# A norm step behind later PSUM copies, Q and K chunks in alternation, and a logit group three steps later, in a one-core transformer kernel

## The chip, the cores and the metric

The kernel runs on one core of one Trainium2 chip. The metric is device time in microseconds (us), lower is better. All times are medians of several executions.

The engines are called as the profile calls them. PE is TensorE (matrix products), DVE is VectorE (elementwise work, sums along a row), ACT is ScalarE (activation functions, here also the copies out of PSUM and most of the layer norm), POOL is GpSimd, and SP is SyncE, which issues DMAs. PSUM is the memory that TensorE writes to.

## The reference, cut to what matters

The input is 2048 tokens of width 1024 in bf16. Two layers, A and B, are applied twice with the same weights.

```python
x = A_x
for _ in range(2):                                    # written out in the original
    x = x + attention(layernorm(x), wqkv, wo)         # 32 heads of 32, window of 8 keys, dilation 2
    x = x + (relu(n @ W_gate) * (n @ W_up)) @ W_down  # n = layernorm(x), F = 3584
```

Attention looks only at the eight keys at distances 0, 2, ..., 14, so its logits are not a large matrix product. They are elementwise products of Q with eight shifted copies of K, summed over each head's 32 features.

## The kernel before

The kernel works on blocks of 512 tokens: four in each of two passes, numbered 0 to 7 in time. Every piece of work is an event with a nominal time. The events are sorted by it and emitted in that order, so that each engine is given its own instructions in this order. The nominal time is therefore a position in a queue, not a wait:

```python
for _, _, f in sorted((at, i, f) for i, (at, f) in enumerate(events)):
    f()
```

`tc.issue_after(ins)` puts an instruction behind `ins` in that order; TensorE's matmul groups are kept in sequence by it. One pool of six PSUM buffers, `acc`, serves the results of all projections.

The layer norm of most blocks runs on ScalarE in two events for each tile of 128 tokens. GpSimd computes a power between two of the ScalarE steps:

```python
def stats(t):
    ...
    nc.scalar.activation(xn, xt[:], ACT.Square, accum_out=sq)
    nc.scalar.activation(xn, xt[:], ACT.Identity, accum_out=sx)
    ...                                                              # three small ScalarE steps -> vpe
    nc.gpsimd.tensor_tensor(rstd, vpe, neg_half[:, 0:1], op=ALU.pow) # variance ** -0.5
    nc.scalar.activation(mr, sx, ACT.Copy, scale=-1.0 / D)
    nc.scalar.activation(nb, mr, ACT.Identity, scale=rstd)           # the bias step: needs GpSimd's result

def apply(t):
    nc.scalar.activation(hold["xn"][:, t, :], x_tiles[b * TPB + t][:], ACT.Identity,
                         scale=hold["st"][:, t, 4:5], bias=hold["st"][:, t, 6:7])
```

The Q and K projections run two Q chunks ahead of K. ScalarE copies each chunk out of PSUM. GpSimd copies the halo, the 14 last tokens of the block before:

```python
QK_ORDER = [("q", 0), ("q", 1)]
for c in range(2, KC):
    QK_ORDER += [("q", c), ("k", c - 2)]
QK_ORDER += [("k", KC - 2), ("k", KC - 1)]
...
    nc.scalar.copy(q[:], acc[:])                 # or k
    ...
    nc.gpsimd.tensor_copy(k[:, 0:HALO], khalo[n - 1][:, c, :])      # L362, blocks after the first
    nc.gpsimd.tensor_copy(khalo[n][:, c, :], k[:, BLK:BLK + HALO])  # L363
```

In block 0 VectorE multiplies each Q chunk with eight shifts of its K chunk (`prod`, L391), and TensorE sums each product over the heads with a selection matrix (the logit matmuls, `L<-prod,sel`). VectorE then computes the softmax, whose exponential (`d<-d`) is ScalarE's. In the later blocks VectorE also sums the eight products (`ac`, `t`, and at last `s`), and TensorE needs one group of eight logit matmuls (`L<-s,sel`). In block 1 that group and its softmax lie inside the gated unit of block 0:

```python
ev.append((t_gu0 + 48.1, red1))                  # the logit matmuls of block 1
ev.append((t_gu0 + 48.2, lambda: softmax(1)))
...
spread(pv_steps(1), at + 58.0, 5.5)              # value products of block 1, at = t_gu0
ev.append((at + 105.0, store_o(1)))              # to DRAM, and back transposed: oT
ev.append((at + 105.1, load_o(1)))
```

The gated unit takes 28 steps of a gate group and an up group, eight matmuls each. ScalarE applies ReLU to the gate (`r`, three buffers), and VectorE multiplies (`hT`). In the down projection four accumulators are filled for one half of the columns, VectorE adds them to the residual (`x<-dacc,x`), and the second half follows. With six `acc` buffers the third accumulator of the second half needs one that these additions free.

## Time and profile before

Three runs took 1642.17 to 1643.27 us, median 1643.09. The profiled execution spans 1640.5 us from its first instruction to its last.

The first part of the profile's page lists each engine's busy time, share of the span and number of instructions:

```profile
PE 1617.3 (99%) x7527; PEld 777.7 (47%) x7576; DVE 1061.3 (65%) x923; ACT 508.1 (31%) x1047; POOL 268.0 (16%) x220
```

TensorE is busy all the time that the profile can see. What is left to win are its holes. The table of waits names what TensorE waited for. Its columns are total microseconds, number of times, and the longest time:

```profile
PE tp L295 <- DVE xn_first L277: 9.1, 1, 9.1
PE L L118 <- DVE s L429: 1.9, 1, 1.9
PE L L118 <- DVE prod L391: 1.7, 2, 0.9
PE tp L295 <- ACT xn_first L292: 1.2, 2, 0.9
PE acc_v L118 <- ACT xnT_first L299: 1.1, 1, 1.1
PE acc_u L118 <- ACT r L550: 1.0, 1, 1.0
PE acc_u L118 <- DVE hT L551: 0.7, 1, 0.7
PE acc_g L118 <- ACT r L550: 0.2, 1, 0.2
```

The lines with `tp` and `acc_v` are the head of the kernel, before 15.3 us: the first norm and its transposes. The change doesn't touch them. The other five lines are six holes with 5.62 us in all:

| hole at (us) | size (us) | stage | waits for |
|---|---|---|---|
| 63.73, 69.54 | 0.85, 0.89 | end of block 0's Q/K stage | VectorE's products |
| 165.96 | 0.69 | gated unit of block 0 | a PSUM buffer that VectorE's hT frees |
| 171.55, 174.48 | 0.25, 1.04 | gated unit of block 0 | PSUM buffers that ScalarE's ReLU frees |
| 202.76 | 1.90 | gated unit of block 0 | the sum s for block 1's logit group |

Why is ScalarE late with a ReLU when it is busy for only 31% of the span? Its timeline shows it. The columns are start, duration, engine, line, operation and tile; the brackets hold the idle time before it and what ended that:

```profile
66.32 0.29 ACT L232 ACTIVATE st_a<-st_a 128x1 f32<-128x1 f32 x1 [1.64 <-POOL st_a L230]
66.52 0.57 ACT L358 CAST k<-acc_k 128x512 bf16<-128x512 f32 x1
...
75.67 1.04 ACT L446 ACTIVATE d<-d 128x1024 f32<-128x1024 f32 x1
...
158.40 0.60 ACT L550 ACTIVATE r<-acc_g 128x512 bf16<-128x512 f32 x1
166.17 0.29 ACT L232 ACTIVATE st_a<-st_a 128x1 f32<-128x1 f32 x1 [7.17 <-POOL st_a L230]
```

L232 is the bias step. It handles 128 numbers in 0.29 us, but at 166.17 it had held up ScalarE for 7.17 us and at 66.32 for 1.64 us, and ReLUs and copies stood behind it. The Trainium skill, "Perfetto Trace Analysis", section "Tensor Engine Instruction (MATMUL, LD_WEIGHTS)", says that ScalarE, VectorE and GpSimd take their instructions strictly in order. This trace agrees: nothing overtook the bias step in those 7.17 us. GpSimd's timeline of the same kernel says why its results were late:

```profile
63.69 2.60 POOL L230 TENSOR_TENSOR st_a<-st_a,neg_half 128x1 f32<-128x1 f32 x1
...
165.44 0.20 POOL L362 COPY k<-kh 128x14 bf16<-128x14 bf16 x1 [21.64 <-DVE ac L417]
165.59 0.55 POOL L230 TENSOR_TENSOR st_a<-st_a,neg_half 128x1 f32<-128x1 f32 x1
```

At 165.44 a halo copy had waited 21.64 us for VectorE, and the power (L230) stood behind it in GpSimd's queue. At 63.69 the power itself took 2.60 us instead of 0.55.

The last two excerpts of before are of VectorE and TensorE. The last product of block 0 starts at 67.17, after a wait for ScalarE's copy of K. The sum s ends at 202.71, and TensorE waited 1.90 us for it:

```profile
67.17 2.31 DVE L391 TENSOR_TENSOR prod<-q,k 128x4096 bf16<-128x4096 bf16 x1 [1.30 <-ACT k L358]
...
200.43 2.28 DVE L429 TENSOR_TENSOR s<-ac,t 128x2048 bf16<-128x2048 f32 x1
```

```profile
198.65 1.89 PE L118 MATMUL acc_u<-xnT_b,w_u 128*128 128x512 bf16 x8
200.47 0.40 PE L118 MATMUL L<-s,sel 128*32 128x512 bf16 x4
202.76 0.40 PE L118 MATMUL L<-s,sel 128*32 128x512 bf16 x4 [1.90 <-DVE s L429]
```

Groups of eight matmuls that run back to back start 1.727 us apart, yet one is drawn 1.89 us long. The same section of the Trainium skill says that the profiler estimates the end of a matmul.

### The profile page before, as it was taken

To read this page: it belongs to the slowest core of one execution; us is meant where nothing else is said; L and a number is where in the kernel's file an instruction comes from. 1 tells how busy PE (TensorE), PEld (TensorE's weight loads), DVE (VectorE), ACT (ScalarE), POOL (GpSimd) and SP (SyncE) were. 2 spreads that over 40 slices of the span, in tenths; PEclk is the share of its full clock that TensorE was granted. 3 is DMA by queue.
4 is the path that set the end of the run, shared out by engine and by line. 5 is a ranking of instruction groups with operands and counts; after the bars stand their busy time and mean duration, and the time that the engine had idled before them with its cause. 6 is when DMAs were issued, how large, how long until landed. Compare 5 with 4: busy or idle time off the path is not lost.

```text
span 1640.5 us, 18585 instructions
## 1 busy us (share of the span) xinstructions
PE 1617.3 (99%) x7527; PEld 777.7 (47%) x7576; DVE 1061.3 (65%) x923; ACT 508.1 (31%) x1047; POOL 268.0 (16%) x220
## 2 busy tenths in 40 slices
PE   7999999999999999999999999999999999999999
PEld 4554345444554445444454444544445444444444
DVE  3699998977298945949369492794928948211211
ACT  5833412424231512415134151340513411131110
POOL 1320205301052102101052010520105100000000
PEclk9999999999999999999999999999999999999999
DMA  8559566746657475774847748577485774755451
GB/s 291 98 152 252 164 180 205 192 146 180 205 177 210 134 199 167 202 200 154 228 153 192 174 154 231 176 183 205 150 225 167 200 213 154 206 154 180 154 164 67
DMA packets 371222, 296.81 MB, mean 181 GB/s; under 512 B 142400, under 2 KB 351296, under 8 KB 370240
## 3 DMA queue, kind: packets, MB, share of 16 engines
q1 hardware_dynamic: 370848, 295.10, 62.7%
q8 instruction: 59, 0.97, 0.3%
q10 hardware_dynamic: 288, 0.52, 0.1%
q14 instruction: 27, 0.22, 0.0%
HBM read 256.77 MB, written 21.00 MB: 169 GB/s over the span
## 4 chain that ended last, share of the span: by engine, by line
PE 93%; DVE 3%; ACT 2%; DMA 1%; issue 1%; POOL 0%; SPq 0%; DVEq 0%; ACTq 0%
PE dacc L118 23%; PE acc_g L118 22%; PE acc_u L118 22%; PE acc_wo L118 7%; PE acc_v L118 6%; PE acc_k L118 6%; PE acc_q L118 6%; DVE t L417 1%; DVE ac L429 1%; DMA x<-in_A_x_dram 1%; DMA v_d<-vT 1%; ACT xn_a L225 0%; ACT xn_a L226 0%; DVE prod L391 0%; PE L L118 0%
## 5 line engine op out<-in xcount | busy, mean ns | idle before, releaser
L118 PE MATMUL acc_u<-xnT_b,w_u 128*128 128x512 bf16 x1792 | 423.3, 379 | 1.7 <-ACT r L550 1.0
L118 PE MATMUL acc_g<-xnT_b,w_g 128*128 128x512 bf16 x1792 | 423.4, 379 | 0.2 <-ACT r L550 0.2
L118 PE MATMUL dacc<-w_d,hT 128*128 128x512 bf16 x1759 | 386.3, 379 | 1.7
L551 DVE TENSOR_TENSOR hT<-acc_u,r 128x512 bf16<-128x512 f32 x224 | 153.3, 687 | 307.4 <-PE acc_u L118 296.1
L550 ACT ACTIVATE r<-acc_g 128x512 bf16<-128x512 f32 x224 | 132.4, 594 | 695.4 <-PE acc_g L118 675.5
L118 PEld LDWEIGHTS <-w_u 128*128 128x128 bf16 x1792 | 175.3, 98 | 213.5 <-issue 2.3
L118 PEld LDWEIGHTS <-w_g 128*128 128x128 bf16 x1792 | 174.7, 98 | 213.0 <-issue 3.3
L118 PEld LDWEIGHTS <-hT 128*128 128x128 bf16 x1792 | 175.3, 98 | 211.4
L419 DVE TENSOR_TENSOR t<-q,k 128x2048 f32<-128x2048 bf16 x84 | 191.7, 2290 | 9.7 <-ACT k L358 7.0
L429 DVE TENSOR_TENSOR ac<-ac,t 128x2048 f32<-128x2048 f32 x84 | 191.7, 2283 | 0.5
L363 POOL COPY kh<-k 128x14 bf16<-128x14 bf16 x64 | 83.8, 1315 | 439.4 <-ACT k L358 439.4
L578 DVE TENSOR_TENSOR x<-dacc,x 128x512 bf16<-128x512 f32 x64 | 42.5, 687 | 164.7 <-PE dacc L118 164.7
L481 DVE TENSOR_TENSOR pv<-a,vhm 128x4096 bf16<-128x4096 bf16 x64 | 145.2, 2282 | 0.0
L230 POOL TENSOR_TENSOR st_b<-st_b,neg_half 128x1 f32<-128x1 f32 x29 | 62.8, 2169 | 319.7 <-ACT st_b L229 319.7
L118 PE MATMUL acc_wo<-w_o,oT 128*128 128x512 bf16 x496 | 111.0, 379 | 0.8
L230 POOL TENSOR_TENSOR st_a<-st_a,neg_half 128x1 f32<-128x1 f32 x32 | 45.9, 1434 | 334.0 <-ACT st_a L229 331.6
L362 POOL COPY k<-kh 128x14 bf16<-128x14 bf16 x48 | 70.2, 1463 | 65.4 <-DVE t L419 43.8
L118 PEld LDWEIGHTS <-oT 128*128 128x128 bf16 x512 | 50.0, 98 | 60.4
L482 DVE TENSOR_TENSOR pv<-pv 128x2048 bf16<-128x2048 bf16 x64 | 77.5, 1215 | 0.2
L319 ACT CAST vT<-acc_v 128x512 bf16<-128x512 f32 x64 | 37.5, 586 | 73.9 <-PE acc_v L118 73.9
L225 ACT ACTIVATE xn_b<-x 128x1024 bf16<-128x1024 bf16 x29 | 30.3, 1045 | 93.1 <-DVE x L526 93.1
L354 ACT CAST q<-acc_q 128x512 bf16<-128x512 f32 x64 | 37.5, 585 | 69.3 <-PE acc_q L118 69.3
(125 smaller groups left out, 1207.5 us busy)
## 6 DMA issues: line engine op xcount, KB each, us to landing
w_g<-in_B_W_gate_dram SPq DMA_DIRECT2D x56, 1024.0 KB, 7.0
w_u<-in_B_W_up_dram SPq DMA_DIRECT2D x56, 1024.0 KB, 5.4
w_d<-in_B_W_down_dram SPq DMA_DIRECT2D x48, 1024.0 KB, 5.8
w_o<-in_A_wo_dram SPq DMA_DIRECT2D x16, 1024.0 KB, 7.3
vhm<-v_d SPq DMA_DIRECT2D x32, 284.0 KB, 6.8
v_d<-vT SPq DMA_DIRECT2D x8, 1024.0 KB, 10.3
oT<-o_d SPq DMA_DIRECT2D x32, 256.0 KB, 4.3
w_d<-in_B_W_down_dram SPq DMA_DIRECT2D x16, 512.0 KB, 3.9
```

The costliest lines, as they stand in the source:

```text
L118: tail_pe[0] = nc.tensor.matmul(*args, **kwargs).ins
L230: nc.gpsimd.tensor_tensor(rstd, vpe, neg_half[:, 0:1], op=ALU.pow)
L319: nc.scalar.copy(st["vT"][:, c, :], acc[:])
L362: nc.gpsimd.tensor_copy(k[:, 0:HALO], khalo[n - 1][:, c, :])
L363: nc.gpsimd.tensor_copy(khalo[n][:, c, :], k[:, BLK:BLK + HALO])
L419: nc.vector.tensor_tensor(t[:], i0, i1, op=ALU.mult)
L429: nc.vector.tensor_tensor(o, ac[:], t[:], op=ALU.add)
L481: nc.vector.tensor_tensor(tt[:], a_bc, v_sh, op=ALU.mult)
L482: nc.vector.tensor_tensor(tt[:, 0:4], tt[:, 0:4], tt[:, 4:8], op=ALU.add)
L550: nc.scalar.activation(r[:], acc[:], ACT.Relu)
L551: nc.vector.tensor_tensor(hold["hT"][:, j, :], accs["u"][:], r[:], op=ALU.mult)
L578: nc.vector.tensor_tensor(xs, ac[t], xs, op=ALU.add)
```

## The change

The change has three parts, called A, B and C below. No work goes or comes.

- **A, the norm.** The bias step leaves `stats` and goes next to `apply`. Both are placed behind the latest ScalarE copy out of PSUM or ReLU, and at later times. A wait for GpSimd should then hold up fewer copies.
- **B, the alternation.** In block 0 the chunks go q0, k0, q1, k1, ..., so that VectorE can start its products earlier.
- **C, the logit group.** Block 1's logit group, its softmax and the value products behind it move later in the gated unit: the group by 10 us, which is three steps of 3.45 us.

The core of the diff; the lines that only record `tail_act[0] = nc.scalar...(...).ins` on the copies of v, q and k and on the ReLU are cut to one:

```diff
 # A
-                sx, sq, nm2, vpe, rstd, mr, nb = (hold["st"][:, t, i:i + 1] for i in range(7))
+                sx, sq, nm2, vpe, rstd, mr = (hold["st"][:, t, i:i + 1] for i in range(6))
...
-                nc.scalar.activation(nb, mr, ACT.Identity, scale=rstd)
...
-                nc.scalar.activation(hold["xn"][:, t, :], x_tiles[b * TPB + t][:], ACT.Identity,
-                                     scale=hold["st"][:, t, 4:5], bias=hold["st"][:, t, 6:7])
+                rstd, mr, nb = (hold["st"][:, t, i:i + 1] for i in range(4, 7))
+                with tc.issue_after(tail_act[0]):
+                    nc.scalar.activation(nb, mr, ACT.Identity, scale=rstd)
+                    nc.scalar.activation(hold["xn"][:, t, :], x_tiles[b * TPB + t][:], ACT.Identity, scale=rstd, bias=nb)
...
-                        nc.scalar.activation(r[:], acc[:], ACT.Relu)
+                        tail_act[0] = nc.scalar.activation(r[:], acc[:], ACT.Relu).ins
...
-        spread(apply, at + 2.0 * gap, gap)
+        spread(apply, at + (2 * gap if dve else max(3 * gap, 12.0)), gap)
...
-            ev.append((a + 4.0, apply[t]))
+            ev.append((a + (4.0 if n == 0 else 12.0), apply[t]))
...
-    ln1(2, 38.0, t_qk1 + 2.0, True, 5.0)
+    ln1(2, 37.0, t_qk1 + 2.0, True, 4.5)
 # B
+    QK_FIRST = [(nm, c) for c in range(KC) for nm in ("q", "k")]
-        return [f_(nm, c) for nm, c in QK_ORDER]
+        return [f_(nm, c) for nm, c in (QK_FIRST if n == 0 else QK_ORDER)]
...
-        ev.append((t_qk0 + GAP0 * (K_STEP[c] + 1.0), mults[c]))
+        ev.append((t_qk0 + GAP0 * (2 * c + 2.0), mults[c]))
-            ev.append((t_qk0 + GAP0 * min(K_STEP[c] + 3.5, 2 * KC - 0.4), reds[c]))
+            ev.append((t_qk0 + GAP0 * (2 * c + 4.5), reds[c]))
 # C
-    ev.append((t_gu0 + 48.1, red1))
-    ev.append((t_gu0 + 48.2, lambda: softmax(1)))
+    ev.append((t_gu0 + 58.1, red1))
+    ev.append((t_gu0 + 58.2, lambda: softmax(1)))
...
-            spread(pv_steps(1), at + 58.0, 5.5)
+            spread(pv_steps(1), at + 66.0, 5.5)
```

More of the change, by code (lines that the diff above doesn't have):

```diff
@@ L96 @@
     tail_sp = [None]
+    tail_act = [None]
     gate = [None]
@@ L318, in f @@
                            start=(kc == 0), stop=(kc == KC - 1))
-                nc.scalar.copy(st["vT"][:, c, :], acc[:])
+                tail_act[0] = nc.scalar.copy(st["vT"][:, c, :], acc[:]).ins
             return f
@@ L353, in f @@
                     q = qk_pool.tile([P, BLK], BF16, tag="q", name=f"q_{n}_{c}")
-                    nc.scalar.copy(q[:], acc[:])
+                    tail_act[0] = nc.scalar.copy(q[:], acc[:]).ins
                     st[("q", c)] = q
@@ L357, in f @@
                     k = qk_pool.tile([P, HALO + BLK], BF16, tag="k", name=f"k_{n}_{c}")
-                    nc.scalar.copy(k[:, HALO:HALO + BLK], acc[:])
+                    tail_act[0] = nc.scalar.copy(k[:, HALO:HALO + BLK], acc[:]).ins
                     if b == 0:
```

## The prediction

> **What bounds the kernel now.** TensorE. The page gives PE 1617 us busy of a span of 1640.5; in its timeline a group of eight 128x512 matmuls starts every 1.727 us, so 7424 of them take about 1602 us (estimate from that step). The Trainium skill, "Perfetto Trace Analysis", "Identifying the Most-Contended Engine", says to judge TensorE by matmul FLOPs, not busy share: 124.6 GFLOP at the 78.6 TF/s of its "Roofline" is 1585 us, 97% of the span. The trace agrees: hardly any headroom.
>
> By the table of waits and the timeline, PE idles 11.4 us before 15.3 us (first norm, transposes), which the change doesn't touch, and then 5.6 us in six holes:
> - 0.85 and 0.89 us at 63 and 69 us: block 0's logit matmuls wait for VectorE products;
> - 0.69, 0.25, 1.04 us at 166, 171, 174 us: block 0's gated unit waits for PSUM slots (hT once, ReLU r twice);
> - 1.90 us at 203 us: block 1's logit group waits for its sum s.
>
> After that PE waits for nothing the table names. So the change can win 5.6 us, 0.34%.
>
> **What it removes, adds and moves.** No work goes or comes; instructions move.
> 1. ScalarE's bias step reads a GpSimd result and stood right behind it. ScalarE idles 1.64 us at 64.7 us (GpSimd's power took 2.60 instead of 0.55 us, beside a VectorE product) and 7.17 us at 159 us (GpSimd's queue held by a K halo copy waiting for VectorE). PSUM copies and ReLUs queue behind. Now bias and apply (1.25 us) stand behind later copies, in the gated unit nine ReLUs later. The r waits go. In blocks 0/1 four of eight applies move to a stage where ScalarE is a third busy.
> 2. Q/K alternation starts VectorE's products (2.3 us each) earlier. K's weights landed at 30 us, in time for 33. I expect product 7 about 2 us earlier, both waits gone or under 0.5 us together, and block 0's exponential (75.7 us) about 6 us earlier. VectorE has no slack until 163 us, so its chain shifts by about 5 us, and the hT wait goes.
> 3. Block 1's logit group comes three steps (10.4 us) later; its 1.90 us go. The price: value products of block 1 end about 4 us later (253 -> 257 us); store (8.2 us to landing) and reload (4.3) then end near 271 us, against an output projection that moves from 279 to 273.5. Slack shrinks from over 10 to about 2 us: the likeliest new wait.
>
> **Prediction.** 5.6 us less 0.5 for leftovers: 1643.1 - 5.1 = **1638.0 us**, 80% range **1636.5 to 1641.5**. Faster by over 2%: 0.5%; within 2%: 98.7%; slower by over 2%: 0.8%.
>
> **What would show it.** Waits table: PE's waits for prod, s, r and hT gone, only the head left. Timeline: block 0's gated unit starting near 147.8 us instead of 149.6, block 1's output projection near 273.5 instead of 279.1, from there a constant lead of 5 to 5.6 us; later stages as long as before. ScalarE: no wait on GpSimd of several us near 160. If step 3's price is real, a PE wait on the oT load near 274 us.
>
> **What would make it wrong.** ScalarE still late at product 7 (about 1 us left); VectorE not shifting, so that PE's earlier arrival becomes a longer hT wait; the oT reload late (1 to 4 us); delayed applies making a transpose late in a steady stage, six times over. A new wait of 33 us, needed for over 2%, I see nowhere.

## The result

In rounds that ran both kernels, before took 1642.63 us (1642.16 to 1643.27, four runs) and after 1636.80 us (1636.70 to 1637.64, four runs). The ratio is 0.9965, with a 95% interval of 0.9948 to 0.9983. The outputs were correct here and in all experiments.

The engines' busy times, from the page of after, are the same as before except GpSimd's, which fell by 12 us:

```profile
PE 1616.4 (99%) x7527; PEld 777.6 (48%) x7576; DVE 1060.9 (65%) x923; ACT 507.7 (31%) x1047; POOL 255.7 (16%) x220
```

The table of TensorE's waits of after. The diff shifts line numbers: before's L118, L391 and L550 are L120, L395 and L554 here.

```profile
PE tp L298 <- DVE xn_first L280: 8.8, 1, 8.8
PE tp L298 <- ACT xn_first L295: 1.2, 2, 0.9
PE acc_v L120 <- ACT xnT_first L302: 1.1, 1, 1.1
PE dacc L120 <- DVE x L582: 0.8, 1, 0.8
PE L L120 <- DVE prod L395: 0.5, 1, 0.5
```

The six holes are gone but for one of 0.54 us at a product, and a new one of 0.79 us has come: `dacc`, the down projection of block 0, waits for VectorE's residual additions. By ScalarE's table of waits, the bias steps of the norms ahead of attention (`st_a`) had waited for GpSimd for 31.5 us in 21 places; in after (where the step is L245) they don't wait at all. Those ahead of the gated unit (`st_b`) waited 44.7 us in 26 places before and 18.7 us in 9 in after, where TensorE doesn't notice. In ScalarE's timeline of after, the exponential of block 0 starts at 71.12 instead of 75.67. The ReLUs near 160 us come on time:

```profile
65.58 0.30 ACT L245 ACTIVATE st_a<-st_a 128x1 f32<-128x1 f32 x1
...
71.12 1.06 ACT L450 ACTIVATE d<-d 128x1024 f32<-128x1024 f32 x1 [0.36 <-DVE d L449]
...
160.39 0.58 ACT L554 ACTIVATE r<-acc_g 128x512 bf16<-128x512 f32 x1
```

VectorE's timeline of after:

```profile
65.29 2.29 DVE L395 TENSOR_TENSOR prod<-q,k 128x4096 bf16<-128x4096 bf16 x1 [1.78 <-ACT k L362]
...
195.85 2.28 DVE L433 TENSOR_TENSOR s<-ac,t 128x2048 bf16<-128x2048 f32 x1
...
206.64 0.69 DVE L555 TENSOR_TENSOR hT<-acc_u,r 128x512 bf16<-128x512 f32 x1 [2.76 <-PE acc_u L120]
...
314.30 2.48 DVE L582 TENSOR_TENSOR x<-dacc,x 128x512 bf16<-128x512 f32 x4
```

The last product comes 1.9 us earlier, and the sum s 4.6 us. After s VectorE has nothing to do until the later logit group: 2.76 us are idle here, and 6.97 us between 198 and 211 us with three more gaps. That time is missing later. From 211 us to the additions at 314.30 the timeline shows no further wait of VectorE. In before VectorE still waited 5.42 and 1.16 us there, for copies of K near 260 us: that was its slack.

TensorE's timeline of after, at the logit group and at the new hole:

```profile
206.47 0.62 PE L120 MATMUL L<-s,sel 128*32 128x512 bf16 x8
...
286.45 27.79 PE L120 MATMUL dacc<-w_d,hT 128*128 128x512 bf16 x126
315.03 2.10 PE L120 MATMUL dacc<-w_d,hT 128*128 128x512 bf16 x9 [0.79 <-DVE x L582]
```

The starts of TensorE's stages give the account of where the time came from:

| start of stage (us) | before | after | lead of after |
|---|---|---|---|
| first Q group | 31.53 | 30.95 | 0.58 |
| gated unit of block 0 | 149.57 | 147.66 | 1.91 |
| output projection of block 1 | 279.08 | 272.64 | 6.44 |
| gated unit of block 1 | 341.24 | 335.75 | 5.49 |
| end | 1640.5 | 1635.0 | 5.5 |

From the gated unit of block 1 on the two traces differ by a constant. The account closes: 5.62 us of holes before, less 1.33 after, is 4.29. Four holes fewer, at 0.16 us under a drawn end each, add 0.64. The head adds 0.58. The sum is 5.51 us. The 0.58 us are chance, as the end of the experiments shows: no part of the change touches that stage.

### The profile page after: what moved, and what is told of

The parts are those of the page before. It is cut to its first block, busy times and chain, and to the rows that moved or that the text cites. A ratio compares the mean times of both kernels' runs of the same rounds, so it can differ in the third digit from the quotient of the medians.

```text
span 1635.0 us, 18583 instructions
## 1 busy us (share of the span) xinstructions
PE 1616.4 (99%) x7527; PEld 777.6 (48%) x7576; DVE 1060.9 (65%) x923; ACT 507.7 (31%) x1047; POOL 255.7 (16%) x220
## 4 chain that ended last, share of the span: by engine, by line
PE 92%; DVE 4%; ACT 2%; issue 1%; DMA 1%; POOL 0%; ACTq 0%; SPq 0%; DVEq 0%
PE acc_g L120 24%; PE acc_u L120 24%; PE dacc L120 22%; PE acc_v L120 6%; PE acc_wo L120 6%; PE acc_k L120 5%; PE acc_q L120 5%; DVE t L423 2%; DVE ac L433 1%; DMA x<-in_A_x_dram 1%; ACT xn_a L227 1%; ACT xn_a L228 1%; DVE pv L485 0%; PE L L120 0%; DVE x L530 0%
## 5 line engine op out<-in xcount | busy, mean ns | idle before, releaser
L120 PE MATMUL acc_g<-xnT_b,w_g 128*128 128x512 bf16 x1792 | 423.4, 379 | 0.0
L120 PE MATMUL acc_u<-xnT_b,w_u 128*128 128x512 bf16 x1792 | 423.3, 379 | 0.0
L120 PE MATMUL dacc<-w_d,hT 128*128 128x512 bf16 x1759 | 386.5, 379 | 2.5 <-DVE x L582 0.8
L554 ACT ACTIVATE r<-acc_g 128x512 bf16<-128x512 f32 x224 | 133.5, 596 | 746.9 <-PE acc_g L120 746.7
L120 PEld LDWEIGHTS <-hT 128*128 128x128 bf16 x1792 | 175.3, 98 | 212.4 <-issue 1.1
L120 PEld LDWEIGHTS <-w_g 128*128 128x128 bf16 x1792 | 174.8, 98 | 212.8 <-issue 3.0
L120 PEld LDWEIGHTS <-w_u 128*128 128x128 bf16 x1792 | 175.4, 98 | 211.4
L120 PE MATMUL acc_wo<-w_o,oT 128*128 128x512 bf16 x496 | 111.0, 379 | 0.8
L232 POOL TENSOR_TENSOR st_b<-st_b,neg_half 128x1 f32<-128x1 f32 x29 | 56.5, 1957 | 297.9 <-ACT st_b L231 297.9
L232 POOL TENSOR_TENSOR st_a<-st_a,neg_half 128x1 f32<-128x1 f32 x32 | 40.5, 1273 | 318.1 <-ACT st_a L231 317.9
L120 PEld LDWEIGHTS <-oT 128*128 128x128 bf16 x512 | 50.1, 98 | 60.3
```

Source lines behind the costliest of these rows:

```text
L120: tail_pe[0] = nc.tensor.matmul(*args, **kwargs).ins
L554: tail_act[0] = nc.scalar.activation(r[:], acc[:], ACT.Relu).ins
```

## The experiments

Twelve kernels ran, on three chips, each in five rounds with before beside it. Before's medians in the calls were 1642.99, 1643.08 and 1642.54 us, and its nine runs of a call were up to 2.3 us apart. About 1.1 us of that is a short dip of TensorE's clock that some of its runs have and others not (see "What was chance"). So a difference under about half a microsecond between two medians decides nothing here.

| run | parts | median us (lowest to highest) | less before's median | ratio, 95% interval |
|---|---|---|---|---|
| e1_alternation | B | 1647.22 (1646.67–1647.70) | +4.2 | 1.0025, 1.0012–1.0037 |
| e2_norm | A | 1638.22 (1637.67–1638.59) | −4.8 | 0.9970, 0.9957–0.9984 |
| e3_logit | C | 1640.65 (1640.18–1641.66) | −2.3 | 0.9986, 0.9974–0.9999 |
| e4_no_logit | A+B | 1637.91 (1637.07–1638.12) | −5.1 | 0.9967, 0.9955–0.9980 |
| e5_no_alternation | A+C | 1637.54 (1636.88–1638.08) | −5.5 | 0.9967, 0.9954–0.9979 |
| after_again | A+B+C | 1636.92 (1636.41–1637.80) | −6.2 | 0.9963, 0.9951–0.9976 |
| e7_one_step | A+B, C by one step | 1636.52 (1635.70–1636.79) | −6.6 | 0.9959, 0.9947–0.9972 |
| e8_six_steps | A+B, C by six steps | 1654.48 (1653.45–1655.30) | +11.4 | 1.0070, 1.0056–1.0084 |
| e9_halo_vector | one halo copy moved | 1642.60 (1642.30–1643.06) | +0.1 | 1.0001, 0.9989–1.0014 |
| e11_bias_only | half of A | 1641.42 (1639.44–1642.32) | −1.1 | 0.9991, 0.9978–1.0003 |
| e13_apply_only | the other half | 1641.05 (1640.46–1641.22) | −1.5 | 0.9991, 0.9978–1.0005 |
| e10_two_steps_late_sums | A+B, C by two steps, later sums | 1635.32 (1633.34–1635.56) | −7.2 | 0.9954, 0.9942–0.9967 |

The parts don't add: alone they give −4.8, +4.2 and −2.3 us, a sum of −2.9, but together −5.8 to −6.2. Two theories stood against each other at the start. By the prediction's, the alternation brings block 0's exponential forward and the norm clears the gated unit. By its rival, the norm does both. Neither foresaw that the alternation alone would lose time.

### Each part alone, and all but the logit group

B alone:

```diff
-        return [f_(nm, c) for nm, c in QK_ORDER]
+        return [f_(nm, c) for nm, c in (QK_FIRST if n == 0 else QK_ORDER)]
...
-        ev.append((t_qk0 + GAP0 * (K_STEP[c] + 1.0), mults[c]))
+        ev.append((t_qk0 + GAP0 * (2 * c + 2.0), mults[c]))
...  # and the matching line of the logit matmuls
```

> Only the Q/K alternation of block 0 (part B) on the kernel before. Main theory (holes are tied together by VectorE's chain, so a hole closed early comes back later unless VectorE also moves): ScalarE's work in block 0 is as much as before, so the exponential of block 0 moves by under 1.5 us and VectorE's chain with it. TensorE's waits for prod shrink from 1.7 to about 1 us or less, but the waits for hT, r and s stay (3.9 us) or grow by what was won; gain of the whole kernel under 1 us. Rival (every hole is worth its own length, parts add up): prod waits gone, others as before, gain 1.5 to 2 us.

Both expectations missed: the alternation alone made the kernel slower by 4.2 us. The exponential went from 75.67 to 79.44 us, in the wrong direction. (Between the profiles it is 5.5 us: 3.8 us of the later exponential and 1.7 us of a clock dip, of which more below.) Three excerpts of its trace show how. GpSimd:

```profile
64.51 2.53 POOL L230 TENSOR_TENSOR st_a<-st_a,neg_half 128x1 f32<-128x1 f32 x1
...
71.14 2.53 POOL L230 TENSOR_TENSOR st_a<-st_a,neg_half 128x1 f32<-128x1 f32 x1
```

VectorE, of the same kernel:

```profile
64.32 2.31 DVE L392 TENSOR_TENSOR prod<-q,k 128x4096 bf16<-128x4096 bf16 x1 [1.66 <-ACT k L359]
70.96 2.31 DVE L392 TENSOR_TENSOR prod<-q,k 128x4096 bf16<-128x4096 bf16 x1 [4.32 <-ACT k L359]
```

And ScalarE:

```profile
67.08 0.29 ACT L232 ACTIVATE st_a<-st_a 128x1 f32<-128x1 f32 x1 [1.61 <-POOL st_a L230]
...
70.30 0.57 ACT L359 CAST k<-acc_k 128x512 bf16<-128x512 f32 x1
...
73.71 0.30 ACT L232 ACTIVATE st_a<-st_a 128x1 f32<-128x1 f32 x1 [1.14 <-POOL st_a L230]
...
79.44 1.04 ACT L447 ACTIVATE d<-d 128x1024 f32<-128x1024 f32 x1
```

Read them in order of time. A product starts at 64.32 and ends at 66.63. The power that starts just behind it, at 64.51, ends only at 67.04. ScalarE's bias step stands waiting for it until 67.08, and the copy of the last K chunk behind that comes at 70.30. VectorE has waited 4.32 us for that copy, starts the last product at 70.96, and the same happens again. Up to the exponential such waits cost ScalarE 5.3 us in five places, against 1.8 us in two places in before. TensorE waited 3.70 us for the last product.

The Trainium skill, "SBUF — State Buffer", section "Who interferes with whom", says that a VectorE instruction with two inputs in SBUF contends with a GpSimd instruction that reads SBUF, because they share a pair of ports, and that the pair is locked. The traces agree: the power takes 0.55 us alone and 2.53 to 2.60 us when it starts just behind the start of a product of 2.31 us. In before, e1 and after, every power that starts within one of block 0's products ends 0.40 to 0.42 us after the product does, however late it started. So it waits for the product's end; it is not merely slowed. In this kernel three powers run for 2.53 to 2.54 us, against one of 2.60 us in before, and three of ScalarE's five waits, 3.9 us together, are for those three. The collision itself is harmless once the bias step is elsewhere: in after two powers still meet a product, but no bias step ahead of attention waits for GpSimd. One of the two:

```profile
45.22 2.53 POOL L232 TENSOR_TENSOR st_a<-st_a,neg_half 128x1 f32<-128x1 f32 x1
```

A alone (its diff is part A above):

> Only the norm behind later copies (part A) on the kernel before. Main theory: ScalarE no longer waits for GpSimd (7.17 us at 159 us and 1.64 us at 65 us gone), so the r waits (1.3 us) go; in block 0 the exponential comes about 3 to 5 us earlier, so VectorE's chain shifts and the hT wait (0.7) goes; prod waits about 1 us instead of 1.7. The s wait stays, 1 to 2 us, because TensorE arrives earlier too. Gain 2.5 to 3.5 us. Rival (parts add up): r waits gone only, 1.3 us.

This is nearly the whole gain: −4.8 us, more than the 2.5 to 3.5 us expected. The exponential starts at 71.16 us, as in after (71.12), and the waits of the gated unit for hT and r are gone. The wait for s stays, with 1.68 us, and 2.42 us of waits stay in block 0's Q/K stage.

```profile
71.16 1.06 ACT L449 ACTIVATE d<-d 128x1024 f32<-128x1024 f32 x1 [0.37 <-DVE d L448]
```

That 71.16 and 71.12 agree is partly luck: e2's first projection happened to be 2.1 us shorter than after's (13.81 against 15.91 us). Counted from the start of the first Q group, the exponential comes after 44.14 us in before, 47.99 with B alone (e1), 42.19 with A alone (e2), 40.63 with A and C (e5, where C acts only later) and 40.17 in after. So A brings 2.0 to 3.5 of the 4.0 us.

C alone (its diff is part C above):

> Only the logit group of block 1 three steps later (part C) on the kernel before. Main theory: wait for s (1.9) gone, prod, hT and r waits as before; value products of block 1 end about 5 to 8 us later (near 261 us), and a wait of the second half of the first down stage for VectorE's residual adds appears, 0.5 to 1.5 us. Gain 0.5 to 1.5 us. Rival (parts add up): s wait gone and no new wait, gain 2 us.

The wait for s goes (1.90 us), and the wait at `dacc` comes (0.78 us). All other holes stay as they were. The profile's span is 2.0 us shorter, and 0.87 us of that are a lead at the gated unit that C cannot have caused. So C alone is worth about 1.1 us in the trace; the medians say 2.3, outside the 0.5 to 1.5 us expected, with an interval that nearly touches 1. Part of that is the clock: all five runs of e3 have 1.000, and against the four runs of before at 1.000 in its rounds (median 1642.38) it is 1.7 us.

A and B without C:

> The changed kernel without part C (logit group back in its old place). Main theory: s is done near 198 us as in the changed kernel, TensorE arrives there near 196.2: a wait for s of 1.5 to 2 us; the new wait of the down stage for the residual adds (0.8) is gone since the value products end near 250 us. So it is about 1 us slower than the changed kernel, near 1637.7, and part C is worth only about 1 us net. Rival (VectorE's shift of 4.6 us by itself makes s early enough): no wait for s, and without the down stage's wait it is 1 us faster than the changed kernel.

It took 5.1 us off, 0.3 us more than A alone, which is inside the spread. TensorE still waits 1.70 us for s.

### A chain through VectorE sets the time

The single profiles show a regularity that explains these sums. In every kernel in which TensorE waits for s, the times from the exponential of block 0 on are fixed distances apart:

| run | exponential of block 0 starts | s ends | gated unit of block 1 starts | span |
|---|---|---|---|---|
| e1 (B) | 79.44 | 206.50 | 346.71 | 1646.0 |
| before | 75.67 | 202.71 | 341.24 | 1640.5 |
| e9 (halo copy) | 74.67 | 201.66 | 341.88 | 1641.1 |
| e13 (half of A) | 74.31 | 201.35 | 339.88 | 1639.1 |
| e11 (half of A) | 73.14 | 200.18 | 338.71 | 1638.0 |
| e2 (A) | 71.16 | 198.17 | 336.70 | 1636.0 |
| e4 (A+B) | 70.81 | 197.84 | 336.37 | 1635.6 |

From the exponential to the end of s it is 127.0 to 127.1 us in each: VectorE works through value products, hT and the sums of block 1 with hardly a gap. From s to the gated unit of block 1 it is 138.53 us in five of them; in e1 and e9 it is 140.2, because TensorE's clock dipped after the wait (shown below). After that all are alike. So in these kernels TensorE's earlier holes set nothing. If TensorE reaches the logit group earlier it waits longer for s. What counts is when ScalarE gets to the exponential.

This tells what C is for. C moves the logit group off the end of this chain. Then TensorE's own stream is the limit, and every hole that A and B close there counts.

### Does closing a hole pay while TensorE still waits for s?

In before, one halo copy in GpSimd's queue caused the wait of 7.17 us. This kernel changes only that copy:

```diff
-                        nc.gpsimd.tensor_copy(k[:, 0:HALO], khalo[n - 1][:, c, :])
+                        (nc.vector if (n, c) == (2, 0) else nc.gpsimd).tensor_copy(k[:, 0:HALO], khalo[n - 1][:, c, :])
```

> The kernel before with one 128x14 copy, the first K halo copy of block 2, moved from GpSimd to VectorE; nothing else. In the kernel before, that copy waits 21.6 us at the head of GpSimd's queue for VectorE's read of the old K buffer and holds up the norm's powers behind it. Expected by every theory: ScalarE's wait of 7.2 us for GpSimd at 159 us falls below 2 us and TensorE's r waits (1.3 us) go. What tells apart: main theory (TensorE's early holes are absorbed at the logit group of block 1, whose sum s comes from VectorE's own unbroken chain, done at 202.7 us): s does not move, the wait for s grows from 1.9 to about 3.3 us, the whole gains under 0.5 us. Rival (a closed hole is time won): gain of 1.3 to 1.7 us.

The table of TensorE's waits of this kernel, without the head:

```profile
PE L L118 <- DVE s L429: 2.8, 1, 2.8
PE L L118 <- DVE prod L391: 1.7, 2, 0.9
...
```

Both waits for r are gone, 1.29 us in before. The wait for s grew from 1.90 to 2.78 us, and the time did not move: 1642.60 against 1642.54. A clock dip behind the longer wait, which this profile has, could hide a gain; but the two runs of e9 at a clock of 1.000 (1642.30 and 1642.60) are no faster than before's four in the same rounds (1641.15 to 1642.50), and s still ends 127.0 us after the exponential. The hole of 7.17 us on ScalarE, the most striking line of the profile before, was worth nothing by itself.

### Which half of A

The bias step next to `apply`, at the old times and without the ordering:

```diff
-                nc.scalar.activation(nb, mr, ACT.Identity, scale=rstd)     # in stats
...
+                nc.scalar.activation(nb, mr, ACT.Identity, scale=rstd)     # in apply, before the big step
```

> Part A cut down: the bias step stands beside the apply, at the old times, without the ordering behind later copies. If the distance from the GpSimd power were all that counts, it does as well as part A alone (1638.2 us, exponential at 71.2 us). Main theory (ScalarE's load before block 0's exponential counts, and in the gated unit the bias must also stand behind ReLUs): the eight applies of 1.25 us still precede the exponential, which comes near 74 us; in the gated unit the bias stands one ReLU ahead of where it would be harmless, so ScalarE still waits about 6 us near 160 us. Gain 0.5 to 2.5 us of part A's 4.8.

And the other half: `apply` late and ordered, the bias step left behind the power in `stats`:

```diff
+                with tc.issue_after(tail_act[0]):
+                    nc.scalar.activation(hold["xn"][:, t, :], x_tiles[b * TPB + t][:], ACT.Identity, scale=rstd, bias=nb)
...
-        spread(apply, at + 2.0 * gap, gap)
+        spread(apply, at + (2 * gap if dve else max(3 * gap, 12.0)), gap)
...  # and the other two times of part A
```

> Part A cut down the other way: the applies are late and ordered behind copies, the bias stays right behind the GpSimd power. Main theory: four applies (5 us) leave the time before block 0's exponential, which comes at 72 to 73.5 us, with ScalarE's waits for GpSimd still in place; the wait of 7 us at 159 us and the r waits stay, but VectorE's chain is earlier, so s is done near 199.5 us. Gain 2 to 4 us. Rival (the stall behind GpSimd is the whole of part A): gain under 1 us.

The halves gave −1.1 and −1.5 us by the medians, and both intervals include 1; the two together give −4.8. The traces say why neither is enough. With the bias step moved but early, ScalarE still waits for GpSimd, 4.39 us at 164 us. With only `apply` moved it waits 1.60 us at 51 us, 3.28 us at 70 us and 5.01 us at 165 us. The exponential starts at 73.14 and 74.31 us, against 71.16 with both. For e13 the expected 72 to 73.5 us and gain of 2 to 4 us were both missed. e11's runs were two near 1639.5 and three near 1641.7, and its profile is of one of the fast ones. The two levels go with the clock: the fast two have 1.000, the other three 0.998 to 0.999. Against before's runs at 1.000 in these rounds (mean 1641.92), e11's two gain 2.4 us and e13, whose runs all have 1.000, gains 0.9.

### The change without B, and the change again

> The changed kernel without part B (Q/K in the old order in block 0). Theory after the first four runs: the exponential of block 0, which starts VectorE's long chain, is set by ScalarE's load, and part A alone had moved it from 75.7 to 71.2 us, as far as all three parts together; so the alternation has little left to give. Expected: exponential near 71 us, waits for prod 1 to 1.7 us instead of 0.5, otherwise as the changed kernel, and 0 to 1 us slower than it. Rival (the prediction's step 2: the alternation is what brings product 7 and the exponential forward): exponential back near 75 us, 3 us or more slower than the changed kernel.

> The changed kernel again, in the same rounds as its variants, for comparison: 1636.8 us, waits for prod 0.5 and for the residual adds 0.8, give or take the first projection, whose length differed between single profiles (13.8 to 16.2 us from its first matmul to the first Q matmul) whatever the kernel.

These ran with e7 and e8. Without the alternation it was 0.6 us slower than the whole change (1637.54 against 1636.92), with ranges that overlap. One hole for a product is 1.01 us there, against 0.50 us, and the exponential starts at 72.45 instead of 71.12; 0.87 us of that is the first Q group, which came later by chance (31.82 against 30.95). So B is worth some tenths once A stands, and costs 4.2 us without it. The second run of after repeats the first: 0.9963 and 0.9965.

### How far to move the logit group

One step later instead of three:

```diff
-    ev.append((t_gu0 + 58.1, red1))
-    ev.append((t_gu0 + 58.2, lambda: softmax(1)))
+    ev.append((t_gu0 + 51.6, red1))
+    ev.append((t_gu0 + 51.7, lambda: softmax(1)))
...
-            spread(pv_steps(1), at + 66.0, 5.5)
+            spread(pv_steps(1), at + 60.0, 5.5)
```

> The changed kernel with the logit group of block 1 one gated-unit step later instead of three. Main theory: the new wait of the first down stage (0.8 us) is there because VectorE idled for the late logit group, and falls away; s is done near 198 us and the group now comes near 199.5, so no wait for s; value products end near 251 us. About 1 us faster than the changed kernel, near 1636. Rival (the down stage waits because TensorE now arrives earlier than VectorE's rate allows): the wait of 0.8 us stays and the time equals the changed kernel's.

The wait at `dacc` is gone, and no wait for s comes back. VectorE starts the residual additions 1.7 us earlier than in after (314.30):

```profile
312.60 2.48 DVE L582 TENSOR_TENSOR x<-dacc,x 128x512 bf16<-128x512 f32 x4
```

So the new wait comes from the size of the move. It is in all three kernels with a move by three steps that were profiled apart from after (e3, e5, after_again: 0.77 to 0.79 us) and in none without it. In time the step is worth 0.4 us by the medians, which the spread does not separate.

Six steps later, with the store and the reload of block 1's attention output behind it:

```diff
-    ev.append((t_gu0 + 58.1, red1))
+    ev.append((t_gu0 + 68.5, red1))
...
-            spread(pv_steps(1), at + 66.0, 5.5)
-            ev.append((at + 105.0, store_o(1)))
-            ev.append((at + 105.1, load_o(1)))
+            spread(pv_steps(1), at + 76.4, 5.5)
+            ev.append((at + 116.0, store_o(1)))
+            ev.append((at + 116.1, load_o(1)))
```

> The changed kernel with the logit group six steps later, value products, store and reload of block 1 moved with it: the suspected cost doubled. Main theory: VectorE idles some 10 us more before that group; all of it comes back as waits of TensorE: 3 to 6 us for the reload before the output projection of block 1, the rest for the residual adds in the first down stage; 8 to 11 us slower than the changed kernel. Rival (only the reload matters, as the prediction had it): a wait for the reload of 3 to 6 us and the down stage's wait as in the changed kernel or less.

This kernel shows the price that the prediction had feared. First TensorE's table of waits of this kernel, then VectorE's last value product and SyncE's issues:

```profile
PE acc_wo L120 <- DMA oT<-o_d: 16.4, 1, 16.4
```

```profile
281.54 0.41 DVE L488 TENSOR_TENSOR ohm<-pv 128x512 bf16<-128x512 bf16 x1
```

```profile
281.97 0.34 SPq L109 DMA_DIRECT2D o_d<-ohm  x1
285.84 2.89 SPq L109 DMA_DIRECT2D oT<-o_d  x4
```

The value products end at 281.9 us instead of 258.0, since they now alternate with block 2's products on VectorE. Store and reload follow, and TensorE stands still for 16.4 us. The mechanism was expected of the reload, but its size was not: 3 to 6 us had been given to it, and 8 to 11 us to the whole, which is 17.6 us slower than the changed kernel. The wait for the residual additions did not come at all, as the rival had it; TensorE reaches them so late here that this does not test it. At three steps the reload was issued at 261.92 us and TensorE needed it only at 272.64.

### A version that beats both

The last kernel takes A and B, moves block 1's logit group by two steps, and also lets the logit matmuls of block 0 come one Q or K group later, against the last hole for a product:

```diff
-            ev.append((t_qk0 + GAP0 * (2 * c + 4.5), reds[c]))
-    ev.append((t_qk1 + 0.5 * GRP, reds[KC - 2]))
-    ev.append((t_qk1 + 1.5 * GRP, reds[KC - 1]))
-    ev.append((t_qk1 + 1.6 * GRP, lambda: softmax(0)))
+            ev.append((t_qk0 + GAP0 * (2 * c + 5.5), reds[c]))
+    ev.append((t_qk1 + 1.5 * GRP, reds[KC - 2]))
+    ev.append((t_qk1 + 2.5 * GRP, reds[KC - 1]))
+    ev.append((t_qk1 + 2.6 * GRP, lambda: softmax(0)))
...
-    ev.append((t_gu0 + 58.1, red1))
+    ev.append((t_gu0 + 55.1, red1))                  # the softmax 0.1 later
...
-            spread(pv_steps(1), at + 66.0, 5.5)
+            spread(pv_steps(1), at + 62.5, 5.5)
```

> An attempt to beat the changed kernel: logit group two gated-unit steps later instead of three, and in block 0 each logit matmul group one Q/K group later. Expected: wait for prod (0.5) gone, wait of the down stage for the residual adds (0.8) gone, exponential of block 0 about 1 us later (72 us), s done near 199 us and the group only at 202 us, so no wait there. No wait of TensorE left after the head; about 1.5 us faster than the changed kernel, near 1635.4. If VectorE's later start matters after all, a wait for residual adds of up to 0.5 us stays.

Its whole table of TensorE's waits is the head:

```profile
PE tp L298 <- DVE xn_first L280: 8.7, 1, 8.7
PE tp L298 <- ACT xn_first L295: 1.2, 2, 0.9
PE acc_v L120 <- ACT xnT_first L302: 1.1, 1, 1.1
```

It took 1635.32 us, 7.2 us under before in its rounds. It ran in another call than after, which was 5.8 and 6.2 us under before in its two. The five runs (1633.34 to 1635.56) lie below all nine of after (1636.41 to 1637.80), but a direct comparison on one chip was not made.

### What was chance

Two effects in single profiles belong to no part. The first projection is the same in all kernels, 64 matmuls, yet took 13.81 us in e2 and e4 and 15.2 to 16.4 us in the others. In before it ran 5, 6 and 8 matmuls in the first three stretches of 2 us from 15 us on, and 11 from then on; in e2 it ran 9 and then 11. The Trainium skill, "TensorE: Matmul & The Clock Gate", section "What's actually happening", says that an idle TensorE runs at half its clock until about 3.4 us of activity have passed, and that the window of this runs freely, so that its cost varies from run to run. The traces agree in kind, with up to 2.6 us between profiles. Most of such a lead is lost again in block 0: e2 led before by 2.56 us at the first Q group, and by 0.92 us at block 1's.

The other effect is a dip of the clock after some holes. A window of e9; the columns are window, length, busy time and instructions of PE, PEld, DVE, ACT and POOL, the granted clock, DMA share and GB/s:

```profile
200.00:210.00 10.00, 8.29 (x33) 3.37 (x33) 7.80 (x8) 2.14 (x3) 0.00 (x0) 0.83 0.00 1
```

After the wait of 2.78 us for s the mean clock of these 10 us was 0.83, which cost 1.7 us. In windows of 2 us it was 0.65 from 202 us on, 0.50 from 204 us and 1.00 again from 206 us. e1 dipped twice, after its waits of 3.70 and 1.90 us. In the profiles of e11 and before, a wait of 2.78 us and one of 1.90 us were followed by none.

The clock listed for every run shows the same over all runs. In the eight kernels whose longest wait of TensorE after the head was 1.77 us or less in the profile (e2, e3, e4, e5, e7, e10, e13 and after, counted with after_again), all 44 runs have 1.000. In before, e1, e8, e9 and e11, where it was 1.90 us or more, 34 of the 47 runs of the experiments have 0.999 or less. Such runs of before took about 1.1 us longer than its others (means 1643.47 against 1642.31 us in the first call, 1643.00 against 1641.92 in the third). So by closing the wait for s the change seems to save these dips too, and the medians gain a little more by it than the two profiles, neither of which has a dip. No run varied the length of a wait alone, so that the length decides is not shown.

## Why the prediction was right or wrong

The time was right: 1638.0 us predicted, 1636.80 and 1636.92 measured, inside the range. Point by point:

- **What bounds the kernel: right.** TensorE's stream is the limit, and the 5.6 us of holes, with about 1 us more under drawn ends (an estimate, six times 0.16), were all there was to win: e10, which closes all six, is 6.7 us shorter than before in its profile. The prediction's sum was 5.6 less 0.5 for leftovers, 5.1. The profiles' difference is 5.5. The leftovers were mis-sized, 1.33 us instead of 0.5. Two terms that the sum did not have made up for it, by luck: 0.64 us hidden under drawn ends of matmuls, and 0.58 us of chance in the head. The medians gained more, 5.8 and 6.2 us, partly because before's runs have clock dips and after's have none.
- **Step 1, the norm: right in direction, too small in size.** The waits for r went, and so did ScalarE's waits for GpSimd near 66 and 160 us. But the step was credited with the r waits only. Alone it gives −4.8 us, most of the gain, because it also brings the exponential forward, by 3.2 us (e5) to 4.5 us (e2).
- **Step 2, the alternation: the step that failed.** "Q/K alternation starts VectorE's products earlier" was to bring product 7 forward by 2 us and the exponential by 6. Product 7 did come 1.9 us earlier, and the exponential 4.55. But A does most of this, and B alone does the opposite: with A alone the exponential starts at 71.16 us, with B alone at 79.44, and beside A the alternation brings about 0.5 us (40.17 against 40.63 us from the first Q group). Earlier products collide with GpSimd's power, and as long as the bias step stands behind the power, that stops ScalarE. The collision was in the profile before (2.60 instead of 0.55 us at 63.69 us, beside a product), and the prediction quoted it without asking whether the alternation would make more of it.
- **VectorE's chain: right.** It was to shift by about 5 us, and s came 4.6 us earlier; the hT wait went. What the prediction did not see is that this chain, and not TensorE's earlier holes, set the time as long as the logit group stood at its end.
- **Step 3, the logit group: right about the wait removed, wrong about the place of the new one.** Value products ended at 258 us as expected (257). The reload of oT was not late: the prediction had left it about 2 us of slack, and store to reload took only 3.9 us (258.06 to 261.92) instead of the 8.2 assumed. The new wait came from VectorE's residual additions, 0.79 us at 315 us: VectorE idled 7 us around the later logit group and had no slack left to make it up. The reload wait is real, but it needs a larger move (16.4 us at six steps).
- **Marks in the profile: nearly all as named.** Block 0's gated unit starts at 147.66 us (147.8 predicted), block 1's output projection at 272.64 (273.5), and the lead then stays at 5.49 (5 to 5.6).

What stays open: the share of B beside A (0.3 and 0.6 us in two pairs, both inside the spread), and why some waits of 1.90 us or more are followed by a clock dip and others, equally long, are not.

## What to carry to other kernels

On an engine that executes in order, look for small steps that wait for another engine's result, and let copies that the bottleneck needs go first; this counts more than the step's own time. Before closing a hole of the bottleneck, find the wait that ends last behind it: as long as a chain on another engine ends in a later wait, the hole only moves there. And move a wait no further than it takes, since the idle time that the move leaves on the other engine comes back later in the program.

## What the Trainium skill lacked or had wrong

- "TensorE: Matmul & The Clock Gate" gives an idle window of about 3.4 us before the clock drops, and for shorter idles no length. Here it dipped after shorter waits: to 0.50 for 2 us after a wait of 2.78 us (e9), at a cost of 1.7 us, and in e1 after one of 1.90 us. Equal waits in the profiles of e11 and before had no dip. No run of the kernels whose waits were 1.77 us or less shows one.
- The same page warns that the clock's trace events are unreliable, without a case such as this: the granted clock reads 1.00 for windows in which before's first projection ran 5 and 6 matmuls per 2 us, against 11 later, yet it shows the dips within the kernel.
- "SBUF — State Buffer" names the contention of a two-input VectorE instruction with GpSimd, but no page gives a number for a small GpSimd step: 0.55 us becomes 2.53 to 2.60 us for a 128x1 power that starts just behind the start of a product of 2.31 us, and it ends 0.40 to 0.42 us after the product.
- "Perfetto Trace Analysis" says that the end of a matmul is estimated. It does not draw the consequence that idle times of TensorE are then understated, here by 0.16 us for each hole (groups start 1.727 us apart and are drawn 1.89 us long).
- No page says that closing a wait can be worth nothing while a later wait hangs on another engine's chain: 1.29 us closed in e9, 0 gained.
